# Another first phase for a fused attention and max-out kernel: order, weights' conversion, join of groups and first softmax

## The chip, the cores and the metric

The kernel runs on one core of a Trainium2 chip. The core has a matrix engine (PE, whose weight loads are shown apart as PEld), a vector engine (DVE), a scalar engine (ACT), a general engine (POOL) and a queue engine (SP) that here starts the transfers. Each engine works through a list of its own, in order, and waits where an instruction needs what another engine has not yet made. The metric is the device time of one execution in microseconds (us): 817.84, the median of three runs (817.79 to 818.44).

## What is computed

Four batches of 12544 tokens with 128 channels go through an attention with 32 learned queries, then through a feed-forward layer that takes the largest of three products. Cut to what matters:

```python
I = broadcast(inducing, (B, 32, 128))
def mab(q, kv):
    s = scale * (q @ kv.T); s = s - s.max(-1)
    a = exp(s); a /= a.sum(-1) + 1e-09
    return a @ kv
h = mab(I, x)                 # 32 states per batch, over all 12544 tokens
y = mab(x, h)                 # every token looks at the 32 states
f = max(y @ w1, y @ w2, y @ w3)   # 128 -> 768
out = f @ w_out                   # 768 -> 128
```

x is float32. The four weights are float64; the kernel reads their two 32-bit words (low, high) and makes float32 of them on the chip.

## The kernel before

A batch's 98 tiles of 128 tokens are seven groups: group 0 has 2 tiles, groups 1 to 6 have 16. Because `y @ w` is `a @ (h @ w)`, the kernel multiplies the 32 states with the weights once per batch (tile `us`, taken apart into a high and a low half so that a fast product keeps its digits) and then works on chunks of at most 512 tokens. For each chunk there are six steps ("slots"), one for each 128 of the 768 middle channels. In a slot PE makes `pu` (product with w1 - w2) and `pv` (with w3 - w2), ACT makes `ru = max(pu, 0)`, DVE makes `h = max(pv, ru)`, ACT casts h to `hi`, POOL (for a few slots DVE) makes `lo = h - hi`, and six slots later PE adds three products with w_out's two halves to the chunk's accumulator `acc`. `pu` and `pv` have two banks each, `ru` has three buffers. One call of `advance` (L813) issues pu of one slot, pv of the one before, and relu, cast and maximum in their turn.

All that comes before is the first phase: the four weights have to be converted, and the first batch's states computed, before the first slot can start. For each group k of the first batch the steps are: load x (SP), transposes in four pieces (T, PE, L282), copies of these from PSUM (c, ACT, L288), scores (S, L298), maximum over the tokens (M, DVE, L308), spread of the maximum over the four quarters (D on ACT, G on PE), least (L, DVE, L327; maxima are kept negated), exponential (E, ACT, L338), its transpose (R, DVE, L352), sum of x with these weights (U, PE, L366) and a copy of the sum (H, ACT, L379). Then the groups are joined: each sum is scaled by the factor of its own maximum (K, `add_group`, on POOL and DVE), two products bring them together (`pa`, `sum`, L610), and the state hT comes out of one DVE product (L635).

A weight is converted in six passes over 128 x 768 words (`convert`, L182; `measure`, L177, squares the high word on ACT to find numbers too small to keep): shift, sign, exponent, low word times exponent, sum (POOL for w1 and w3, DVE for w2 and w_out), and a product that clears the small ones. Then w1 - w2 and w3 - w2 (L219).

The order of all this is written by hand: `STEPS1` (L43) is a list of steps that are issued one after the other, each of which puts its instructions at the end of its engines' lists, `F` being products of an identity that nobody reads. `ORDER` (L55) goes on with the softmax of the first tokens, in two parts (a: group 0 and 4 tiles of group 1, b: the other 12 tiles of group 1), the first products with the weights, and the first seven calls of `advance` (s); S there is the scores of group 2. From then on `main` (L1044) goes from slot to slot by a plan. In slot 8 the plan has the first scores for the second batch (`turn_products`, L389).

LOADS (L41) is the order of the transfers: 0 to 6 are groups of x, 7 is w2, 8 w_out, 9 w1, 10 w3.

## Time and profile before

| | |
|---|---|
| median of three runs | 817.84 us |
| span of the profiled execution, first to last instruction | 816.4 us |
| PE busy | 806.8 us (99%) |
| ACT busy | 720.2 us (88%) |
| POOL busy | 658.8 us (81%) |
| DVE busy | 653.4 us (80%) |
| granted clock of PE | 1.000 |

Times in the rows are us from the first instruction of that execution. The median of the runs stands 1.4 us above its span. A share of busy time is a mean over very different stretches: the first 55 us are one piece of work that happens once, the other 760 us repeat the slot. A step of the first phase is found in the timeline by its line. PE's fp32 products show as two records for each, and the pieces of one tile are merged in a row with their count (x8 for eight transposes).

### The profile page before, as it was taken

Reading aid. Unit: us, or ns where it says so; the run is one execution under the profiler, and the core shown is the slowest. Engines: PE = TensorE matmul, PEld = TensorE weight load, DVE = VectorE, ACT = ScalarE, POOL = GpSimd, SP = SyncE. Lnnn points to the kernel's source line nnn. Section 1 sums busy time; section 2 is a strip of 40 time slices with the busy share of each in tenths; the row PEclk is TensorE's granted clock in tenths of the full one; section 3 lists DMA queues with packets and bytes.
Section 4 is the critical chain, followed back from the end, with each engine's and each line's share of the span. In section 5 each row is a group of like instructions: output and inputs, shape, how many; then the busy total and the mean of one; then the engine's idle time right before and its main releaser. Section 6 shows DMA issues by size and latency. Waiting matters only on the chain.

```text
span 816.4 us, 14999 instructions
## 1 busy us (share of the span) xinstructions
PE 806.8 (99%) x4565; PEld 628.9 (77%) x4565; DVE 653.4 (80%) x1198; ACT 720.2 (88%) x1446; POOL 658.8 (81%) x640
## 2 busy tenths in 40 slices
PE   8999999999999999999999999999999999999998
PEld 5667778777787787777777877877778778777886
DVE  5989778787797797887986978878789878878874
ACT  5779889898898898988988988989889999999996
POOL 0369898798798987987989888879878888878886
PEclk9999999999999999999999999999999999999999
DMA  9335643543553435435453354343231222222221
GB/s 345 140 149 160 192 150 107 182 125 105 155 175 123 129 107 176 124 112 177 128 166 112 114 167 124 110 126 124 60 108 56 83 65 79 69 81 75 62 78 52
DMA packets 45408, 101.47 MB, mean 124 GB/s; under 512 B 9360, under 2 KB 15376, under 8 KB 40208
## 3 DMA queue, kind: packets, MB, share of 16 engines
q1 hardware_dynamic: 45184, 100.39, 39.1%
q8 instruction: 36, 0.59, 0.3%
q14 instruction: 44, 0.36, 0.1%
q10 hardware_dynamic: 144, 0.13, 0.0%
HBM read 48.12 MB, written 25.69 MB: 90 GB/s over the span
## 4 chain that ended last, share of the span: by engine, by line
PE 94%; DVE 3%; ACT 1%; issue 1%; DMA 1%; POOL 0%; SPq 0%; DVEq 0%
PE acc L908 49%; PE pv L826 16%; PE pu L820 16%; PE aux L708 3%; PE acc L904 3%; PE acc L486 2%; PE aux L389 2%; DVE h L858 1%; DMA xg<-in_x_dram 1%; POOL rest L208 0%; PE pv L282 0%; PE pu L282 0%; PE aux L298 0%; PE aux L670 0%; ACT ru L835 0%
## 5 line engine op out<-in xcount | busy, mean ns | idle before, releaser
L850 POOL TENSOR_TENSOR lo<-h,hi 128x512 fp32r<-128x512 f32 (+1 forms) x498 | 624.8, 1284 | 109.3 <-ACT hi L842 58.4
L858 DVE TENSOR_TENSOR h<-pv,ru 128x512 f32<-128x512 f32 (+1 forms) x524 | 349.9, 672 | 131.2 <-PE pv L826 106.7
L835 ACT ACTIVATE ru<-pu 128x512 f32<-128x512 f32 (+1 forms) x600 | 365.3, 609 | 66.8 <-PE pu L820 61.8
L842 ACT CAST hi<-h 128x512 fp32r<-128x512 f32 (+1 forms) x524 | 326.5, 623 | 3.0 <-DVE h L858 2.2
L908 PE MATMUL acc<-hi,wo_hi 128*128 128x512 f32 (+1 forms) x601 | 235.1, 391 | 0.0
L826 PE MATMUL pv<-pT,us 128*128 128x512 f32 (+1 forms) x600 | 233.0, 389 | 1.0 <-DVE h L858 0.8
L820 PE MATMUL pu<-pT,us 128*128 128x512 f32 (+1 forms) x600 | 231.8, 386 | 0.1
L908 PE MATMUL acc<-hi,wo_lo 128*128 128x512 f32 (+1 forms) x601 | 231.5, 385 | 0.0
L908 PE MATMUL acc<-lo,wo_hi 128*128 128x512 f32 (+1 forms) x601 | 231.4, 385 | 0.0
L908 PEld LDWEIGHTS acc<-hi,wo_hi 128*128 128x128 f32 x601 | 112.8, 188 | 41.8 <-issue 20.5
L826 PEld LDWEIGHTS pv<-pT,us 128*128 128x128 f32 x600 | 112.6, 188 | 28.6 <-DVE h L858 5.5
L820 PEld LDWEIGHTS pu<-pT,us 128*128 128x128 f32 x600 | 112.6, 188 | 24.5 <-ACT ru L835 1.7
L908 PEld LDWEIGHTS acc<-lo,wo_hi 128*128 128x128 f32 x601 | 112.8, 188 | 23.0
L908 PEld LDWEIGHTS acc<-hi,wo_lo 128*128 128x128 f32 x601 | 112.9, 188 | 21.8
L858 DVE TENSOR_TENSOR aux<-pv,ru 128x512 f32<-128x512 f32 x66 | 45.9, 695 | 11.6 <-PE pv L826 4.5
L861 DVE TENSOR_TENSOR lo<-aux,hi 128x512 fp32r<-128x512 f32 x66 | 45.4, 688 | 0.8 <-PE acc L908 0.8
L842 ACT CAST hi<-aux 128x512 fp32r<-128x512 f32 x66 | 40.5, 614 | 0.3
L920 ACT COPY shelf<-acc 128x512 f32<-128x512 f32 (+1 forms) x65 | 39.0, 600 | 0.0
L904 PE MATMUL acc<-pT,us 128*128 128x512 f32 (+1 forms) x100 | 38.8, 388 | 0.0
L208 POOL TENSOR_TENSOR rest<-rest,t 128x768 f32<-128x768 f32 x2 | 3.7, 1826 | 28.7 <-DVE rest L204 23.6
L430 POOL COPY mq<-mq 32x1 f32<-32x1 f32 (+2 forms) x108 | 20.4, 189 | 5.2
L708 PE MATMUL aux<-xT,hT 128*32 128x512 f32 x184 | 24.5, 605 | 0.0
(169 smaller groups left out, 561.6 us busy)
## 6 DMA issues: line engine op xcount, KB each, us to landing
out_dram<-shelf SPq DMA_DIRECT2D x95, 256.0 KB, 2.0
xg<-in_x_dram SPq DMA_DIRECT2D x22, 1024.0 KB, 5.8
xT<-in_xt_dram SPq DMA_DIRECT2D x18, 1024.0 KB, 5.1
pT<-ph SPq DMA_DIRECT2D x184, 64.0 KB, 2.0
pT<-pl SPq DMA_DIRECT2D x184, 64.0 KB, 2.0
raw<-in_w_dram SPq DMA_DIRECT2D x3, 768.0 KB, 13.5
us<-uh SPq DMA_DIRECT2D x24, 52.0 KB, 2.4
us<-ul SPq DMA_DIRECT2D x24, 52.0 KB, 1.9
```

The lines of the kernel that those rows point to most:

```text
L430: nc.gpsimd.tensor_copy(out=far[to : to + step], in_=own[lo : lo + step])
L708: nc.tensor.matmul(out=sp[q * M : (q + 1) * M, :w], lhsT=st["hT"][:, :M], rhs=xT[:, q * w : (q + 1) * w], start=True, stop=True)
L820: nc.tensor.matmul(out=pu[:, :w], lhsT=state[c.b]["us"][:, 2 * j * P : (2 * j + 1) * P], rhs=c.pT[:, :w], start=True, stop=True)
L826: nc.tensor.matmul(out=pv[:, : d.w], lhsT=state[d.b]["us"][:, (2 * j + 1) * P : (2 * j + 2) * P], rhs=d.pT[:, : d.w], start=True, stop=True,)
L835: nc.scalar.activation(out=ru[:, :w], in_=pu[:, :w], func=AF.Relu)
L842: nc.scalar.copy(out=hi[:, : c.w], in_=h[:, : c.w])
L850: nc.gpsimd.tensor_sub(**args)
L858: nc.vector.tensor_max(out=h[:, : d.w], in0=pv[:, : d.w], in1=relus.pop(s)[:, : d.w])
L861: nc.vector.tensor_sub(**low)
L904: nc.tensor.matmul(out=c.acc[:, :w], lhsT=us[:, 2 * DF :], rhs=c.pT[:, :w], start=True, stop=False)
L908: nc.tensor.matmul(out=c.acc[:, cs], lhsT=lhs[:, j, :], rhs=rhs[j][:, cs], start=False, stop=(j == NJ - 1 and rhs is c.hl and cs.stop == w),)
L920: (nc.vector.tensor_copy if by_vector else nc.scalar.copy)(out=o[:, : c.w], in_=c.acc[:, : c.w])
```

## The change

The hand-written lists `STEPS1` and `ORDER` are replaced by one list, `HEAD`, which also runs slots 0 to 7; `main` starts at slot 8. What the list issues changes too:

- Weights: the high word's size is taken by Abs on ACT (`weight_size`, n), DVE makes a small number of the low word (`weight_rest`, r), raises the size to a least value (`weight_least`, m) and shifts its bits (`weight_shift`, i), POOL adds the two as whole numbers (`weight_whole`, v; all four weights), and DVE puts the sign on (`weight_sign`, d).
- Transfers: groups 1 and 2 come ahead of w2, and w_out is the last of the eleven (it was the fifth).
- Unread products: 17 at the start and none until the first products with the weights; then, in a bank of `pv`, ten of 256 columns in six pieces, before and between the first calls of `advance` (N).
- Copies: four of the copies of transposed x (C) and one copy of a group's sum (HV, group 1) go from ACT to DVE; all seven sums are kept in SBUF.
- Join: one product makes seven masks from the factors (`combine_masks`, DVE), and seven small products on PE (`combine_group`, y) add the groups; the adds on POOL and DVE go.
- First softmax: three parts (A: group 0, B: 4 tiles of group 1, C: the other 12), the first and second chunk's probabilities being turned by `probs_turn` and copied by DVE and ACT.
- The scores of group 2 go from `ORDER` into the plan, to slot 8.

Three places of the lists show what moves. First PE's list from its first instruction, where acc<-ident_r is an unread product, pu and pv the banks of the transposes, xg_86 group 1 and xg_87 group 2. Before:

```order
L274 MATMUL acc_76<-ident_r 128x384 x4
L282 MATMUL pu_72<-shelf 128x128 x2
L274 MATMUL acc_76<-ident_r 128x384
L298 MATMUL aux_70<-shelf 32x64 x4
L274 MATMUL acc_76<-ident_r 128x384 x2
L321 MATMUL acc_76<-md,shelf 128x4
L282 MATMUL pu_72<-shelf,xg_86 128x128 x4
L282 MATMUL pu_73<-shelf,xg_86 128x128 x4
L282 MATMUL pv_74<-shelf,xg_86 128x128 x4
L282 MATMUL pv_75<-shelf,xg_86 128x128 x4
L274 MATMUL acc_76<-ident_r 128x384 x2
L298 MATMUL aux_71<-xT_78,shelf 32x512 x4
```

After:

```order
L271 MATMUL acc_76<-ident_r 128x384 x17
L279 MATMUL pu_72<-shelf 128x128 x2
L279 MATMUL pv_74<-shelf,xg_86 128x128 x4
L279 MATMUL pv_75<-shelf,xg_86 128x128 x4
L279 MATMUL pu_73<-shelf,xg_86 128x128 x4
L295 MATMUL aux_70<-shelf 32x64 x4
L279 MATMUL pu_72<-shelf,xg_86 128x128 x4
L279 MATMUL pv_74<-shelf,xg_87 128x128 x4
L279 MATMUL pu_73<-shelf,xg_87 128x128 x4
L318 MATMUL acc_76<-md,shelf 128x4
L295 MATMUL aux_71<-xT_78,shelf 32x512 x4
```

The unread products are all ahead of the first transpose, and transposes of group 2 come ahead of the scores of group 1 (aux_71).

Second, PE's list at the first slots, where L820 and L831 are pu, L826 and L837 pv, L789 and L795 the turning of probabilities, and aux_70<-xT,hT the scores of group 2. Before:

```order
L789 MATMUL pu_72<-ident_r,pn 128x128 x2
L649 MATMUL acc_76<-shelf,hT 128x128
L789 MATMUL pu_73<-ident_r,pn 128x128 x4
L820 MATMUL pu_72<-pT,us 128x256
L708 MATMUL aux_70<-xT_79,hT 32x512 x4
L820 MATMUL pu_73<-pT,us 128x256
L826 MATMUL pv_74<-pT,us 128x256
L820 MATMUL pu_72<-pT,us 128x256
L826 MATMUL pv_75<-pT,us 128x256
```

After:

```order
L271 MATMUL pv_74<-ident_r 128x256 x2
L795 MATMUL pu_72<-ident_r,pn 128x128 x2
L657 MATMUL acc_76<-shelf,hT 128x128
L795 MATMUL pu_73<-ident_r,pn 128x128 x4
L831 MATMUL pu_72<-pT,us 128x256
L271 MATMUL pv_74<-ident_r 128x256 x2
L831 MATMUL pu_73<-pT,us 128x256
L837 MATMUL pv_74<-pT,us 128x256
L271 MATMUL pv_74<-ident_r 128x256 x2
L831 MATMUL pu_72<-pT,us 128x256
L837 MATMUL pv_75<-pT,us 128x256
L271 MATMUL pv_74<-ident_r 128x256
```

The scores of group 2 are gone from here, and unread products stand between a pv and the next pu, in the bank of that pv.

Third, ACT's list from the cast of the last softmax part (pn, 128x24x32 values) on, where ru is the relu and hi the cast of h. Before:

```order
L765 CAST pn<-aux_71 128x24x32
L800 CAST pT<-pu_73 128x4x4x32
L835 ACTIVATE ru<-pu_72 128x256
L654 CAST us<-acc_76 128x128
L662 COPY uf<-acc_76 64x128
L835 ACTIVATE ru<-pu_73 128x256
L835 ACTIVATE ru<-pu_72 128x256
L842 CAST hi<-h 128x256
L835 ACTIVATE ru<-pu_73 128x256
L842 CAST hi<-h 128x256
```

After:

```order
L853 CAST hi<-h 128x256
L846 ACTIVATE ru<-pu_73 128x256
L853 CAST hi<-h 128x256
L846 ACTIVATE ru<-pu_72 128x256
L853 CAST hi<-h 128x256
L846 ACTIVATE ru<-pu_73 128x256
L853 CAST hi<-h 128x256
L774 CAST pn<-acc_77 128x24x32
L846 ACTIVATE ru<-pu_72 128x512
L853 CAST hi<-h 128x256
```

The cast of pn stood ahead of the first relu; it now stands between the relus of 256 and of 512 columns.

The diff, cut to its core:

```diff
-LEAST = 2.0**-15 * 1.125
+LEAST = 2.0**-15
...
-    LOADS = (0, 7, 1, 2, 8, 3, 4, 9, 5, 10, 6)
+    LOADS = (0, 1, 2, 7, 3, 9, 4, 5, 10, 6, 8)
...
-    STEPS1 = (
-        "F4 T0.0 c0.0 F1 S0 M0 D0 F2 G0 W0 z0 W0 T1.0 W0 T1.1 c1.0 L0 W0 E0 T1.2 c1.1 R0 T1.3 W0 "
...
+    HEAD = """
+        F:17 T:0.0 T:1.2 T:1.3 T:1.1 C:0.0 S:0 T:1.0 c:1.2 T:2.2 c:1.1 T:2.1 M:0 D:0 G:0 L:0 C:2.1 c:1.3 c:1.0 S:1
...
+        turn:0 pcv:0 up:3 hi:3 turn:1 pca:1 s:0 lop:3 p:2.4 lov:2 N:2 s:1 N:2 s:2 p:2.5 N:1 s:3 N:1 s:4 p:2.6 N:2
+        s:5 p:2.7 next s:6 p:2.8 q:0 q:1 q:2 q:3 q:4 q:5 q:6 q:7
...
-    ORDER = "a a b a a b a b 0 w l a b a a b b 1 2 a b p c b P s X 3 Y S z s s s s s b s"
...
-        size = sizes[k] = hp.tile([P, DF], F32, name="size", tag="size", bufs=2)
-        nc.scalar.activation(out=size, in_=high.bitcast(F32), func=AF.Square)
...
+    def weight_size(k):
         v = raws[k].rearrange("p (k two) -> p two k", two=2)
+        words[k] = v[:, 0, :], v[:, 1, :]
+        sized[k] = hp.tile([P, DF], F32, name="size", tag="size", bufs=2)
+        nc.scalar.activation(out=sized[k], in_=words[k][1].bitcast(F32), func=AF.Abs)
+    def weight_rest(k):
+        rests[k] = hp.tile([P, DF], F32, name="rest", tag="rest", bufs=2)
+        low = raws[k].rearrange("p (k two) -> p two k", two=2)[:, 0, :]
+        nc.vector.tensor_scalar(out=rests[k], in0=low, scalar1=2.0**-51, scalar2=2.0, op0=ALU.mult, op1=ALU.add)
+    def weight_least(k):
+        nc.vector.tensor_scalar(out=sized[k], in0=sized[k], scalar1=LEAST, scalar2=None, op0=ALU.max)
+    def weight_shift(k):
+        bits = sized[k].bitcast(U32)
+        nc.vector.tensor_scalar(out=bits, in0=bits, scalar1=3, scalar2=None, op0=ALU.logical_shift_left)
+    def weight_whole(k):
+        whole = rests[k].bitcast(I32)
+        nc.gpsimd.tensor_tensor(out=whole, in0=whole, in1=sized[k].bitcast(I32), op=ALU.add)
+    def weight_sign(k):
+        floats[k] = wf[:, k, :] if k < 2 else hp.tile([P, DF], F32, name="dst", tag="dst", bufs=2)
+        nc.vector.scalar_tensor_tensor(
+            out=floats[k].bitcast(U32),
+            in0=words[k][1],
+            scalar=0x80000000,
+            in1=rests[k].bitcast(U32),
+            op0=ALU.bitwise_and,
+            op1=ALU.bitwise_or,
         )
...
-            out=t, in0=high, scalar1=3, scalar2=0x3FFFFFF8, op0=ALU.logical_shift_left, op1=ALU.bitwise_and
-            out=t, in0=high, scalar=0xC0000000, in1=t, op0=ALU.bitwise_and, op1=ALU.bitwise_or
-        nc.vector.tensor_scalar(out=pw, in0=t, scalar1=0xFF800000, scalar2=None, op0=ALU.bitwise_and)
-            out=rest, in0=low, scalar=2.0**-52, in1=pw.bitcast(F32), op0=ALU.mult, op1=ALU.mult
-        (nc.gpsimd if k > 1 else nc.vector).tensor_add(out=rest, in0=rest, in1=t.bitcast(F32))
-            out=dst, in0=sizes[k], scalar=LEAST * LEAST, in1=rest, op0=ALU.is_ge, op1=ALU.mult
...
-    def attend_keep(b, gi):
+    def attend_keep(b, gi, copy):
-        nc.scalar.copy(out=st["hg"][:parts, gi, :], in_=st["h"][:parts, :C])
+        copy(out=st["hg"][:parts, GROUPS.index(gi), :], in_=st["h"][:parts, :C])
...
+            "HV": lambda gi: attend_keep(0, gi, vec.tensor_copy),
+            "N": lambda n: unread_products(n, bank_v[0][:, 2 * P :]),
...
+    def combine_masks(st, engine):
+        st["mask"] = bp.tile([P, NG, M], F32, name="mask", tag="mask", bufs=1)
+        engine.tensor_mul(
+            out=st["mask"],
+            in0=sel[:, :M].unsqueeze(1).to_broadcast([P, NG, M]),
+            in1=st["w"].unsqueeze(2).to_broadcast([P, NG, M]),
+        )
...
+    def combine_group(st, at, bank):
+        st["sum"] = bank
+        parts = min(groups[GROUPS[at]]["nt"], NQ) * M
+        nc.tensor.matmul(
+            out=bank[:, :M],
+            lhsT=st["hg"][:parts, at, :],
+            rhs=st["mask"][:parts, at, :],
+            start=(at == 0),
+            stop=(at == NG - 1),
+        )
...
+    PARTS = (("A", groups[0]["nt"]), ("B", TC), ("C", GT - TC))
+
+    def scores_part(which):
 
         st = state[0]
+        gi = int(which > 0)
+        xT, per = st["xT"][gi], groups[gi]["nt"] * M
+        key, bank, a, z = (
+            ("A", bank_v[0], 0, per), ("B", bank_a[0], 0, TC * M), ("C", bank_o[1], TC * M, per)
+        )[which]
...
-        total = (bank_a[0] if gi == "A" else bank_a[1])[:, 512 - GT : 512 - GT + nt]
+        total = sp[:, w : w + nt] if gi in ("A", "B", "C") else bank_a[1][:, 512 - GT : 512 - GT + nt]
...
+    def probs_turn(c, bank):
         src = state[c.b][("p", c.key)]
+        c.pT = wk.tile([P, 512], F32R, name="pT", tag="pT", bufs=4)
+        for t in range(c.w // P):
+            nc.tensor.transpose(
+                out=bank.bitcast(F32R)[:, t * P : (t + 1) * P],
+                in_=src[:, c.base + t, :, :, :].rearrange("p d s m -> p (d s m)"),
+                identity=ident_r,
+            )
...
-            if i > 0:
-                at(s0 + BURST[0], scores_products, b, g + 1, bank_a[0])
+            at(s0 + BURST[0], scores_products, b, g + 1, bank_a[0])
...
-        phase1_first()
...
+        head()
+        main(8)
```

## Rows read from the trace of the kernel before

**Rows 1.** Page: us busy, share of the span and instructions of each engine.

```profile
PE 806.8 (99%) x4565; PEld 628.9 (77%) x4565; DVE 653.4 (80%) x1198; ACT 720.2 (88%) x1446; POOL 658.8 (81%) x640
```

**Rows 2.** Windows: stretch, us, busy PE PEld DVE ACT POOL, clock, DMA, GB/s.

```profile
10.00:25.00 15.00, 14.49 (x128) 9.28 (x127) 11.86 (x19) 11.34 (x25) 0.00 (x0) 1.00 1.02 408
14.90:41.06 26.16, 24.63 (x335) 17.15 (x333) 24.22 (x47) 20.20 (x48) 7.80 (x9) 1.00 0.52 200
41.06:55.27 14.21, 13.51 (x88) 8.32 (x88) 12.48 (x31) 11.30 (x29) 8.13 (x10) 1.00 0.54 211
55.27:75.00 19.73, 19.73 (x110) 14.74 (x111) 17.16 (x35) 17.83 (x37) 18.18 (x20) 1.00 0.26 86
```

**Rows 3.** Chain that ended last: start, us, what; 0 to 70 us.

```profile
24.14 0.97 DVE rest L204
...
25.18 1.84 POOL rest L208
...
51.67 0.28 ACT ru L835
51.95 0.29 ACT hi L842
```

**Rows 4.** Timeline, first feed-forward steps: start, us, engine, line, op, tiles, count.

```profile
47.40 0.80 ACT L765 CAST pn<-aux 128x768 fp32r<-128x768 f32 x1 [0.45 <-DVE aux L759]
...
48.05 1.06 PE L708 MATMUL aux<-xT,hT 128*32 128x512 f32 x8
...
48.57 0.40 ACT L835 ACTIVATE ru<-pu 128x256 f32<-128x256 f32 x1
...
54.53 0.68 DVE L802 CAST pT<-acc 128x512 fp32r<-128x512 f32 x1
...
55.27 0.16 PEld L389 LDWEIGHTS acc<-shelf 128*32 128x32 f32 x8 [0.72 <-DVE pT L802]
```

**Rows 5.** DVE groups, 0 to 48 us: busy us, mean ns, idle before.

```profile
L352 DVE STREAM_TRANSPOSE aT<-a 128x512 f32<-128x512 f32 x6 | 4.2, 707 | 0.5 <-ACT a L338 0.5
L308 DVE TENSOR_REDUCE mq<-aux 128x1 f32<-128x512 f32 x6 | 4.1, 684 | 2.6 <-PE aux L298 2.6
...
L195 DVE SCALAR_TENSOR_TENSOR t<-raw,t 128x768 uint32<-128x768 uint32 x4 | 3.8, 959 | 0.1
L200 DVE TENSOR_SCALAR pw<-t 128x768 uint32<-128x768 uint32 x4 | 2.2, 560 | 0.1
...
L219 DVE TENSOR_TENSOR shelf<-dst,xT 128x768 f32<-128x768 f32 x1 | 1.0, 960 | 0.0
L327 DVE TENSOR_REDUCE mneg<-acc 128x1 f32<-128x4 f32 x6 | 0.9, 156 | 0.2 <-PE acc L321 0.2
```

**Rows 6.** Groups of ACT and POOL, 0 to 48 us, in the same form.

```profile
L288 ACT COPY xT<-pu 128x512 f32<-128x512 f32 x12 | 6.9, 601 | 3.6 <-PE pu L282 3.6
...
L208 POOL TENSOR_TENSOR rest<-rest,t 128x768 f32<-128x768 f32 x2 | 3.7, 1826 | 28.7 <-DVE rest L204 23.6 <-DVE mneg L327 5.1
```

**Rows 7.** Timeline of DVE: the least of group 1, and the state hT.

```profile
14.90 0.16 DVE L327 TENSOR_REDUCE mneg<-acc 128x1 f32<-128x4 f32 x1 [0.25 <-PE acc L321]
...
40.77 0.29 DVE L635 TENSOR_TENSOR hT<-pu,rec 128x128 f32<-128x128 f32 x1
```

**Rows 8.** Timeline of PE: unread products, and runs of eight transposes.

```profile
1.88 1.65 PE L274 MATMUL acc<-ident_r 128*128 128x384 f32 x4 [1.88 <-DVE ident_r L154]
...
7.09 1.97 PE L282 MATMUL pu<-shelf,xg 128*128 128x128 f32 x8 [0.17 <-DMA xg<-in_x_dram]
...
12.95 1.09 PE L282 MATMUL pu<-shelf,xg 128*128 128x128 f32 x8
...
28.88 1.09 PE L282 MATMUL pu<-shelf,xT 128*128 128x128 f32 x8
```

**Rows 9.** DMA issues of 5 to 6 us and of 9.44 to 11 us.

```profile
xg<-in_x_dram SPq DMA_DIRECT2D x1, 1024.0 KB, 11.1
...
xT<-in_x_dram SPq DMA_DIRECT2D x1, 256.0 KB, 17.2
```

More of the change, by code (lines that the diff above doesn't have):

```diff
@@ L11 @@
 U32 = mybir.dt.uint32
-LEAST = 2.0**-15 * 1.125
+I32 = mybir.dt.int32
+LEAST = 2.0**-15
 AF = mybir.ActivationFunctionType
@@ L126, in place @@
         return shelf[:, shelf_at[0] - n : shelf_at[0]]
-    outs = [place(512) for _ in range(OB)]
+    join = place(OB * 512)
+    outs = [join[:, i * 512 : (i + 1) * 512] for i in range(OB)]
     short_t = [place(groups[0]["nt"] * P) for i in range(2)]
@@ L141 @@
     raws = {}
-    FULL = next(gi for gi in LOADS if 0 < gi < NG)
+    FULLS = [gi for gi in LOADS if 0 < gi < NG]
     def first_loads():
@@ L226, with weight_difference @@
+    def weight_difference(k, part, parts, engine):
+        js = range(part * NJ // parts, (part + 1) * NJ // parts)
+        cs = slice(js[0] * P, (js[-1] + 1) * P)
+        engine.tensor_sub(
+            out=wcat[:, : 2 * DF].rearrange("p (j s c) -> p s j c", s=2, c=P)[:, k - 2, js[0] : js[-1] + 1],
+            in0=floats[k][:, cs].rearrange("p (j c) -> p j c", c=P),
+            in1=wf[:, 0, cs].rearrange("p (j c) -> p j c", c=P),
+        )
     w2t = []
@@ new lines, in head @@
+            "pcv": lambda n: probs_copy(chunks[n], bank_u[n], vec.tensor_copy),
+            "s": lambda n: advance(),
+            "q": slot,
+        }
+        for step in HEAD.split():
+            name, *args = step.split(":")
+            args = [int(a) for a in ".".join(args).split(".")] if args else []
+            if name in "TcC" and len(name) == 1:
+                if name == "T":
+                    transpose_x(0, *args)
+                else:
+                    copy_x(0, *args, act.copy if name == "c" else vec.tensor_copy)
+            elif name in ("e", "ep"):
+                weight_difference(*args, vec if name == "e" else pool)
+            elif name == "p":
+                which, n = args
+                if which not in softmax:
+                    softmax[which] = scores_steps(0, *PARTS[which])
+                next(softmax[which])
+            elif name in ("parts", *steps):
+                steps[name](*args)
+            else:
+                raise ValueError(step)
@@ L1107, with main @@
+    def main(first):
+        for s in range(first, len(slots) + LAG + 1):
+            slot(s)
+    with tc.manual_schedule(engines=MANUAL):
+        head()
+        main(8)
 _GT = 16
```

335 lines of the change are left out of this document (119 added, 216 removed), and 7 rows, old and new, of the table STEPS1.

## The prediction

> **What bounds the kernel now.** The page first [rows 1]: PE is busy for 806.8 of 816.4 us, every other engine for under 90%. The windows come next [rows 2]: from 55.27 us on PE has no gap (19.73 of 19.73), so what lies behind 55.27 costs the same however early it starts. A change of the first phase is therefore worth exactly the time by which it moves the product that stands at 55.27 (L389, the first scores of the second batch, slot 8 of the feed-forward steps), as long as PE's list behind it stays the same, and it does. Third, the chain in order of time [rows 3] says what holds that product back. Up to the state hT it runs through the weights' conversion on DVE and POOL (rows at 24.14 and 25.18, and the same again for the next weight); the window 14.90 to 41.06 agrees, with DVE busy 24.22 of 26.16, more than ACT (20.20). From 51 us on the chain alternates between ACT's relu (0.28) and cast (0.29), and in the end stands DVE's copy of probabilities (54.53), which L389 waits for [rows 4]. So there are two stretches: 14.90 to hT's end at 41.06 (DVE), and 41.06 to 55.27 (14.21 us, mostly ACT).
>
> **First stretch: the conversion and the join.** Before, a weight costs DVE two passes of 0.56 (L191, L200) and three of 0.96 (L195, L204, L212), and a fourth of 0.96 (L208) for w2 and w_out; POOL adds for the other two [rows 5, 6]. After, it is three of 0.56 (rest, least, shift) and one of 0.96 (sign): 2.64 for each against 4.96 or 4.00, or 10.6 against 17.9 in all. Against that stand new DVE instructions: of 24 copies of transposed x of 128x512, 3 go from ACT to DVE (0.68 each, as the copy at 54.53 in [rows 4]), one copy of a group's sum (128x128), and one product of 128x224 for the masks, while the joins of L581, L583 and L604 go. Of the old 17.9, w2's whole 4.96 was done before 14.90; of the new passes only one is, since w2 now lands behind two groups of x.
>
> So I count what DVE has to do between the least of group 1 (14.90 before, [rows 7]) and hT, with the durations of [rows 5]: 11 single-input passes at 0.56 = 6.2; 4 sign passes at 0.96 = 3.8; one difference of 128x768 at 0.96 = 1.0; 6 transposes at 0.707 = 4.2; 5 maxima at 0.684 = 3.4; 2 copies at 0.68 = 1.4; 6 least at 0.156 and three of that size = 1.4; and six smaller ones (copy, mask, half a difference, two for the reciprocal, hT's own 0.29) about 2.2. Sum 23.6.
>
> Where does it start? Group 1 no longer stands behind w2 in the queue; PE is with the 17 unread products until about 7.3 (1.88 plus 17 of 384 columns at 1.2 GHz, 0.32 each; the row of four at 1.88 took 1.65 [rows 8]). If the clock is up after them, the 16 transposes of group 1 cost twice 1.09 (row at 12.95) in place of twice 1.97 (row at 7.09): 1.7 us less, of which the start, later by 0.2, and ACT's copies of 0.6 take about half. I put the least of group 1 at 14.1. The later groups don't hold it up: 768 KB less lie ahead of group 3 (issued at 5.08, landing 11.1 later, [rows 9]) and of group 6 (first quarter at 26.6), which is 1.9 us at the 408 GB/s of [rows 2]: 14.3 and 24.7.
>
> 14.1 + 23.6 = 37.7 would be hT's end without any wait. Before, DVE waited for 1.94 us of the 26.16. After, I find waits where the queue stands: the copy of group 1's sum (put on DVE, ahead of the least of group 2) waits for PE's scores of groups 2 and 3 and that sum, and so does all behind it, ACT's weights of group 2 included; the fourth weight's sign, just ahead of hT, waits for POOL's add. About 0.9 in all, so **hT ends at 38.6: 2.45 earlier**. From below it is 37.7 (no wait), from above 39.7 (waits as before). The unknown prices: an integer add on POOL, taken like the fp32 add (1.83), is covered by some 0.5 us of other DVE work for w1, w3 and w_out, so up to 2.3 it costs nothing; Abs in place of Square on ACT and max or shift on DVE keep the shapes of rows at hand and are taken at those; the mask lies between a 128x128 and a 128x384 pass (0.3 to 0.6; I take 0.37, and it is off by at most 0.2).
>
> **Second stretch, hT to L389.** Four terms against the 14.21 of before.
> (a) The cast of the big part's probabilities (0.80, with ACT idle for 0.45 ahead of it, row at 47.40 [rows 4]) no longer stands ahead of the first relu; a copy uf of 512 columns (0.6, as ACT's copies in [rows 6]) is new there. 0.45 + 0.80 - 0.6 = **0.6 gained**.
> (b) That cast now stands between the fourth and fifth cast of h, in the chain of relus and casts that sets this stretch, with nothing to cover it: **0.8 lost**.
> (c) The unread products write the bank of pv that DVE reads for h, so PE's queue stands until h is made, and the next pu is queued behind. The relu for that slot could start when h of two slots before is done (its buffer), now h, two products of 256 columns, pu and the way to ACT come after each other: about **0.65 lost**, once; the second such place is covered by ACT's queue.
> (d) The scores of group 2 (1.06, row at 48.05 [rows 4]) stood where PE waited for the second chunk's probabilities. Now they stand in slot 8, ahead of L389, where PE waited 0.72 for DVE (row at 55.27): 1.06 less the part of that wait which is left, about **0.4 lost**.
> The three softmax parts give nothing more: the first pu needs parts A and B, whose DVE passes interleave with C's.
> Sum: 14.21 - 0.6 + 0.8 + 0.65 + 0.4 = 15.46, so L389 comes at 38.6 + 15.46 = 54.05 and not 55.27: 1.2 us earlier. The profiled execution's span of 816.4 becomes 815.2; the median of the runs, 817.84, stands 1.4 above the span, and with the same 1.4 the forecast is **816.6**. Bounds of the terms: (b) and (c) between 0 (covered) and 0.8 and 1.3 (both places), (d) 0 to 1.06.
>
> **A rule against the change.** The row at 7.09 shows a run of transposes alone, on a PE that had been busy for most of the time since 1.88, at half the rate of the row at 12.95 (the granted clock reads 1.00 in every window, so the level is read from durations); between the two rows stand unread products and scores. The Trainium skill, "TensorE: Matmul & The Clock Gate", Part 4 (PE-mode transpose), says that transposes don't count as busy for the clock the way other products do; the trace agrees as far as that row goes. It is rival 2, whose price comes from the rows alone. Of POOL's add, the Trainium skill, "GPSIMD Engine Reference", Key points, says that POOL shares its SBUF interfaces with DVE and gets into its way in DVE's two-port modes; the add of 1.83 was measured beside such passes, and no row here shows it without.
>
> **Rivals.**
> 1. *Nothing is given back.* The relus and casts still set the pace, but (b), (c), (d) fall into waits that I don't see; hT at 38.6 or a little before. 817.84 - 2.45 = 815.4, with hT at 37.7 814.5; I say 814.9. For it: ACT is at 11.30 of 14.21 in that stretch, so 2.9 us are free. Against: the chain at 51.67 and 51.95 has no gap.
> 2. *The clock falls (slower).* Before, seven pieces of unread products stand among the transposes of the first groups; after, all 17 are ahead of the first transpose and from 7.3 to about 16 PE has almost only transposes, and waits for group 3. If the clock falls there, the 16 transposes of group 3 cost 1.8 more (twice 1.97 for 1.09), the scores of groups 2 and 3 and the sum of group 1 about 0.4 each: 3.0, on the way to DVE's maxima. It decides if the drop lasts beyond 14.3, when group 3 lands; earlier it is hidden by that transfer. 816.6 + 3.0 = 819.6. Against: the transposes at 28.88, with no unread product for many us ahead of them, keep 1.09 for 8, but they have scores and sums around them.
> 3. *The integer add on POOL is slow (slower).* At twice the fp32 price (3.7), w1's sign waits 1.4 longer and w_out's, ahead of hT, 1.4 again: 819.4. From 2.3 it starts to count.
> 4. *It doesn't do what it says:* hT is held by ACT's and PE's turn from maximum to weights, not by DVE; the waits grow by the 1.2 that are left. 817.8.
>
> **Chances.** Forecast 0.45 (own range 815.3 to 817.9), rival 1 0.25, rival 2 0.12, rival 3 0.08, rival 4 0.10. No change means within 0.2%, 1.6 us here: 816.2 to 819.5. Of the forecast's 0.45 some 0.17 lie below 816.2. Faster 0.17 + 0.25 = 0.42; same 0.28 + 0.10 = 0.38; slower 0.20. The range takes in rival 1 with its lower end and reaches to rival 2: 814.4 to 819.6.
>
> **What will show it.** The window from the least of group 1 to hT: hT's end near 38.6, DVE busy there for about 23.6. POOL's integer add at 1.8. The transposes of groups 1 and 3 at 1.1 for 8 (2.0: rival 2). ACT's cast of 128x768 between casts of h, and PE idle in front of the third unread pair with DVE's h as the releaser. L389 near 54. The forecast is wrong if hT stays above 40, or if L389 comes less than 14.5 us after it.

## The result, and the profile after

The changed kernel takes 822.62 us (median of five runs, 819.79 to 824.14) where the kernel before takes 818.2 (817.79 to 818.56): a ratio of 1.0053, 95% interval 1.0043 to 1.0064. It is slower by half a per cent. The forecast was 816.6, and its range ended at 819.6.

The five runs differ by more than those of before, and they differ with PE's mean granted clock, which was 0.998 once and otherwise 0.999 or 1.000 in the runs of the kernel before that were timed beside the experiments:

```
us       819.79  822.51  822.62  823.27  824.14
clock     1.000   0.995   0.996   0.995   0.993
```

The profiled execution is the one of 823.27 (span 821.5). First its windows, in the form of [rows 2]: from the least of group 1 to hT's end, a part of that, a part with a low clock, from hT to the first scores of the second batch (L380, in the kernel before L389), and what follows.

```profile
15.63:41.35 25.72, 24.07 (x328) 18.11 (x328) 23.24 (x45) 18.24 (x45) 7.32 (x4) 0.93 0.51 190
16.00:34.00 18.00, 17.94 (x248) 13.02 (x247) 17.27 (x32) 15.17 (x38) 5.50 (x3) 1.00 0.66 253
37.97:44.80 6.83, 6.45 (x64) 4.14 (x57) 4.50 (x17) 1.44 (x4) 0.00 (x0) 0.50 0.54 170
41.35:59.10 17.75, 16.08 (x99) 10.00 (x103) 12.96 (x37) 12.76 (x33) 9.74 (x11) 0.90 0.47 169
...
59.10:79.00 19.90, 19.90 (x115) 14.87 (x108) 16.69 (x35) 17.74 (x36) 18.04 (x20) 1.00 0.28 87
```

The stretch up to hT ends at 41.35, not at 38.6, and the next one takes 17.75, where the forecast had 15.46 and the kernel before 14.21 [rows 2]. Behind L380 PE has no gap, as before. So L380 comes at 59.10, 3.83 later than in [rows 4], and that is most of the 5.1 by which the span grew. Note that PE was busy for 17.94 of the 18.00 us from 16 to 34.

Then DVE's timeline around hT, and POOL's add (start, us, engine, line, operation, tiles). The product of weights and group sums, `lw`, has seven columns and takes 1.77; it ends when POOL's integer add ends (34.98 + 1.82 = 36.80).

```profile
34.75 0.38 DVE L608 TENSOR_TENSOR mask<-shelf,w 128x224 f32<-128x224 f32 x1
...
35.05 1.77 DVE L627 TENSOR_TENSOR lw<-w,lst 128x7 f32<-128x7 f32 x1
...
41.06 0.29 DVE L643 TENSOR_TENSOR hT<-pu,rec 128x128 f32<-128x128 f32 x1 [1.68 <-PE pu L617]
```

```profile
34.98 1.82 POOL L201 TENSOR_TENSOR rest<-rest,size 128x768 int32<-128x768 int32 x1 [4.22 <-DVE size L197]
```

Two more of DVE's passes are long: `rest` at 18.04 and the sign at 22.88 take 1.15 and 1.46, where the same passes take 0.55 and 0.94 elsewhere. Both start while POOL adds (16.94 to 18.77 and 21.70 to 23.53) and end behind it.

```profile
18.04 1.15 DVE L190 TENSOR_SCALAR rest<-raw 128x768 f32<-128x768 uint32 x1
...
22.88 1.46 DVE L205 SCALAR_TENSOR_TENSOR xT<-raw,rest 128x768 uint32<-128x768 uint32 x1
```

PE's timeline shows the rest: a wait for group 3's transfer at 15.83, a wait for the reduction behind `lw` at 37.07, the sums of one group in 1.08 at full clock and in 1.82 at 37.78, and later the two pieces of unread products (a pair and a single one) that wait for DVE's h.

```profile
15.83 0.66 PE L279 MATMUL pu<-shelf,xg 128*128 128x128 f32 x4 [0.24 <-DMA xg<-in_x_dram]
...
34.47 1.08 PE L359 MATMUL acc<-xg,aT 128*32 128x128 f32 x32 [0.35 <-ACT a L331]
...
37.07 0.41 PE L633 MATMUL acc<-shelf,l 128*128 128x32 f32 x2 [0.40 <-DVE l L629]
37.78 1.82 PE L359 MATMUL acc<-xT,aT 128*32 128x128 f32 x32 [0.30 <-DVE aT L345]
...
51.31 0.51 PE L271 MATMUL pv<-ident_r 128*128 128x256 f32 x2 [0.59 <-DVE h L869]
...
53.05 0.39 PE L271 MATMUL pv<-ident_r 128*128 128x256 f32 x1 [0.64 <-DVE h L869]
```

The granted clock in short windows: PE is busy for 0.65, 1.00 and 0.67 us of the three microseconds from 34, and from 38 on it gets half its clock (1.2 GHz in place of 2.4), until 44.8.

```profile
34.00:35.00 1.00, 0.65 (x22) 1.00 0.00 0
35.00:36.00 1.00, 1.00 (x25) 1.00 0.06 16
36.00:37.00 1.00, 0.67 (x6) 1.00 0.00 0
...
37.50:38.00 0.50, 0.22 (x8) 0.96 0.00 0
38.00:38.50 0.50, 0.50 (x17) 0.50 0.00 0
```

### The profile page after: what moved, and what is told of

Same layout as the page of the kernel before. It is cut to its first block, busy times and chain, and to the rows that moved or that the text cites. A ratio compares the mean times of both kernels' runs of the same rounds, so it can differ in the third digit from the quotient of the medians.

```text
span 821.5 us, 15091 instructions
## 1 busy us (share of the span) xinstructions
PE 809.9 (99%) x4584; PEld 632.4 (77%) x4584; DVE 648.3 (79%) x1200; ACT 717.6 (87%) x1445; POOL 658.9 (80%) x635
## 4 chain that ended last, share of the span: by engine, by line
PE 94%; DVE 3%; DMA 1%; ACT 1%; issue 0%; POOL 0%; SPq 0%; DVEq 0%; ACTq 0%
PE acc L919 49%; PE pv L837 16%; PE pu L831 16%; PE aux L716 3%; PE acc L915 3%; PE acc L477 2%; PE aux L380 2%; DMA xg<-in_x_dram 1%; DVE h L869 1%; PE aux L295 0%; PE acc L359 0%; PE pv L279 0%; DVE aT L345 0%; POOL lo L861 0%; PE aux L678 0%
## 5 line engine op out<-in xcount | busy, mean ns | idle before, releaser
L837 PE MATMUL pv<-pT,us 128*128 128x512 f32 (+1 forms) x600 | 233.5, 389 | 1.1 <-DVE h L869 0.9
L831 PE MATMUL pu<-pT,us 128*128 128x512 f32 (+1 forms) x600 | 231.9, 387 | 0.1
L919 PEld LDWEIGHTS acc<-hi,wo_hi 128*128 128x128 f32 x601 | 112.8, 188 | 41.4 <-issue 20.5
L837 PEld LDWEIGHTS pv<-pT,us 128*128 128x128 f32 x600 | 112.6, 188 | 30.2 <-DVE h L869 7.2
L831 PEld LDWEIGHTS pu<-pT,us 128*128 128x128 f32 x600 | 112.7, 188 | 23.7 <-ACT pT L524 0.3
L915 PE MATMUL acc<-pT,us 128*128 128x512 f32 (+1 forms) x100 | 38.8, 388 | 0.0
L201 POOL TENSOR_TENSOR rest<-rest,size 128x768 int32<-128x768 int32 x4 | 7.3, 1829 | 28.2 <-DVE size L197 28.2
L716 PE MATMUL aux<-xT,hT 128*32 128x512 f32 x184 | 24.5, 605 | 0.0
```

The source lines that it names most:

```text
L716: nc.tensor.matmul(out=sp[q * M : (q + 1) * M, :w], lhsT=st["hT"][:, :M], rhs=xT[:, q * w : (q + 1) * w], start=True, stop=True)
L831: nc.tensor.matmul(out=pu[:, :w], lhsT=state[c.b]["us"][:, 2 * j * P : (2 * j + 1) * P], rhs=c.pT[:, :w], start=True, stop=True)
L837: nc.tensor.matmul(out=pv[:, : d.w], lhsT=state[d.b]["us"][:, (2 * j + 1) * P : (2 * j + 2) * P], rhs=d.pT[:, : d.w], start=True, stop=True,)
L915: nc.tensor.matmul(out=c.acc[:, :w], lhsT=us[:, 2 * DF :], rhs=c.pT[:, :w], start=True, stop=False)
L919: nc.tensor.matmul(out=c.acc[:, cs], lhsT=lhs[:, j, :], rhs=rhs[j][:, cs], start=False, stop=(j == NJ - 1 and rhs is c.hl and cs.stop == w),)
```

## The experiments

The changed kernel's list HEAD can be edited step by step (v is POOL's integer add, i the shift ahead of it, d the sign; 1 stands for w_out). Every kernel below is the changed kernel with the edits shown, timed beside the kernel before. hT is the end of that pass and L380 the start of the first scores of the second batch, both in the profiled execution, with its mean clock; the ratio is that of the times to the kernel before. There is one profiled execution of each kernel, and hT and L380 vary from execution to execution (f4's is the slowest of its twelve, 824.21), so the median says what an edit is worth and the profile why.

```
                        ratio    interval         median   hT     L380   clock
changed kernel          1.0053   1.0043-1.0064    822.62  41.35  59.10   0.995
e1_sum_first            1.0021   1.0012-1.0030    819.71  40.13  57.91   0.997
e2_filler               1.0030   1.0021-1.0040    820.45  39.73  55.89   1.000
e3_no_unread_ffn        1.0024   1.0015-1.0033    820.44  40.76  57.59   0.993
e4_scores_first         1.0063   1.0050-1.0075    823.39  41.32  59.40   0.995
f1_add_early_filler     1.0027   1.0017-1.0036    820.04  41.47  58.00   0.998
f2_and_no_unread_ffn    1.0009   1.0000-1.0018    818.85  41.70  56.76   0.996
f3_and_scores_first     1.0027   1.0019-1.0036    820.21  41.24  56.33   0.998
f4_group2_in_head       1.0003   0.9988-1.0017    817.63  44.92  61.25   0.991
g4_sum_on_pool          1.0015   1.0006-1.0024    818.85  39.88  56.09   0.997
g2_unread_other_bank    1.0045   1.0031-1.0058    820.67  39.77  54.17   0.999
g1_four_edits           1.0002   0.9993-1.0011    818.13  39.32  54.14   0.999
g3_no_unread_ffn        0.9997   0.9989-1.0006    817.65  41.24  55.68   0.998
h3_w2_early             1.0069   1.0049-1.0090    825.24  44.75  62.67   0.996
h2_all_w2_early         1.0022   1.0013-1.0032    819.61  41.81  56.27   0.998
h1_all_scores_first     1.0033   1.0021-1.0045    820.60  42.83  57.28   0.997
```

### Does DVE's lw wait for POOL?

```diff
-i:1 v:1 mask lw w2T
+mask lw i:1 v:1 w2T
```

> Only one pass is moved: the shift of w_out's sizes (0.55 on DVE), and with it the start of POOL's integer add, goes behind the product of weights and group sums (lw, L627). Theory A (DVE's lw, both operands in SBUF, stood still while POOL added): lw takes 0.2 and not 1.77; PE's wait for the sum of the groups (0.40 at 37.07) goes, hT ends at 39.4 (41.35 with the change); if the clock then holds, L380 comes near 55.7 and the time is about 819. Rival (lw is slow by itself, or waits for ACT's weights): lw stays at 1.77 and hT at 41.3, time 822.6. Rival (the clock falls for want of unread products whatever DVE does): lw is short, hT ends near 40, but the granted clock reads 0.50 for some 7 us around 40, time about 821.

`lw` takes 0.16, and the difference that now meets the add takes 1.83 in place of 0.52. POOL ends at 38.22 and the difference at 38.64, nearly its usual length later:

```profile
35.44 0.16 DVE L627 TENSOR_TENSOR lw<-w,lst 128x7 f32<-128x7 f32 x1
...
36.81 1.83 DVE L217 TENSOR_TENSOR shelf<-dst,xT 128x384 f32<-128x384 f32 x1
```

```profile
36.41 1.81 POOL L201 TENSOR_TENSOR rest<-rest,size 128x768 int32<-128x768 int32 x1 [5.54 <-DVE size L197]
```

So the wait belongs to the add, not to `lw`: a pass of DVE with two operands in SBUF that comes while POOL adds stands still until the add is done. (`rest` at 18.04 shows that one of a single operand can stand still too.) Transposes and passes that read PSUM go on beside an add, as in the changed kernel beside the one from 28.92 to 30.75, the second of these lines being a maximum over PSUM:

```profile
29.51 0.71 DVE L345 STREAM_TRANSPOSE aT<-a 128x512 f32<-128x512 f32 x1
30.14 0.65 DVE L305 TENSOR_REDUCE mq<-aux 128x1 f32<-128x512 f32 x1
```

The time of e1 is 2.9 us lower than the changed kernel's; hT is only 1.2 earlier, and behind it, from 40 on, the clock fell in this execution as well (0.55 in the window from 40 to 42).

The other half of the same question takes `lw` off DVE and moves the difference behind the reciprocal, and changes nothing else:

```diff
-i:1 v:1 mask lw w2T ... tot e:3.0.2 rec
+i:1 mask lw v:1 w2T ... tot rec e:3.0.2
-        nc.vector.tensor_mul(out=lw, in0=st["w"], in1=st["lst"])
+        nc.gpsimd.tensor_mul(out=lw, in0=st["w"], in1=st["lst"])
```

> The changed kernel, with the product of weights and group sums (lw, 7 columns) made by POOL ahead of its integer add, and the difference e:3.0.2 behind the reciprocal, so that no pass with two SBUF operands that hT needs meets the add. Nothing else. Theory A: lw about 0.2 on POOL, DVE's transposes of the last group at 35.3 and not 36.94, the difference waits for the add's end (1.0 to 1.5 instead of 0.52) but ends before PE has the last group's sum; hT ends at 38.5 to 38.9, as the prediction had it (38.6). Whether the clock then holds is open: if it does, L380 at 54.9 and time about 817.9; if it falls, 820. Rival (PE's and ACT's turn holds hT anyway): hT not before 40.

hT ends at 39.88, but this execution had its least of group 1 only at 16.51, since the clock fell near 12 us (0.50 in the window from 12 to 14; more of this below). From there the stretch took 23.37. In `g2_unread_other_bank`, which has the changed kernel's code up to hT and kept its clock, it took 24.35 (15.42 to 39.77). Counted from PE's sums of the last group but one (34.26 in g2, 35.32 in g4), hT ends 5.51 and 4.56 later, so the wait of `lw` is worth 0.95 of hT. From g2's start of 15.42 the 23.37 would end at 38.8, an estimate, and that is where theory A had it. The rival was half right: with the wait gone, DVE stands waiting for PE (0.93 ahead of the reciprocal).

Bringing the add forward instead, with four unread products of 384 columns in the idle places:

```diff
-d:3 M:6 D:6 L:5 E:5 U:4 H:4 G:6 r:1 m:1 L:6 E:6 R:5 least wts i:1 v:1 mask lw
+d:3 r:1 L:5 m:1 i:1 v:1 M:6 D:6 E:5 U:4 H:4 G:6 L:6 E:6 R:5 least wts mask lw
-y:1 tot e:3.0.2        ...  y:6 hT
+y:1 X:1 tot X:2 e:3.0.2  ...  y:6 X:1 hT
```

> w_out's rest, least, shift and the POOL add go ahead of the last group's maximum, so that POOL adds beside DVE's maximum and transposes (which read PSUM or have one operand), not beside the mask, lw or a difference; four unread products of 384 stand between the joins. Theory A: lw 0.2, no pass of DVE between 33 and 40 is longer than its usual time, hT ends at 38.3 to 38.9, clock 1.00, L380 16.2 later (54.5 to 55.1); with the 1.3 that all kernels with the change are later behind L380, the time is about 818.7. Rival (the wait only moves on to another pass, as it did with the sum first: mask or difference grows to 1 or more): hT after 39.4, time 819.8 or more.

A miss. No pass of DVE between 33 and 40 is long any more (`lw` 0.16), yet hT ends at 41.47 with the clock at 1.00: the last group's maximum now stands behind 1.7 us of conversion, and PE waits 1.32 for what follows from it.

```profile
34.81 0.39 PE L318 MATMUL acc<-md,shelf 128*128 128x4 f32 x2 [1.32 <-ACT md L311]
```

### What is the clock worth, and what keeps it up?

Seven unread products between the joins ahead of hT, in a bank (aux0) that nobody reads there:

```diff
-y:1 tot e:3.0.2          ...  y:3 y:5 y:6 hT
+y:1 X:2 tot X:2 e:3.0.2  ...  y:3 y:5 X:2 y:6 X:1 hT
+            "X": lambda n: unread_products(n, bank_a[0][:, P:]),
```

> Seven unread products of 384 columns go into PE's list between the joins ahead of hT, in a bank that nobody reads there; lw is left as it is. Clock theory (PE's idle pieces between 34 and 38, 1.4 in all, make the clock fall from 37.97 to 45.3): the granted clock stays 1.00, hT ends at about 39.9 and L380 comes 2.7 to 3.3 earlier than 59.10; time about 819.8, as the one run of the changed kernel whose mean clock read 1.0. Rival (the clock falls for another reason, or PE is still idle for long): clock 0.50 for 7 us again, time 822 to 823. Under both, lw stays at 1.77.

In nine runs the mean clock was never below 0.998 (0.993 to 1.000 in the five of the changed kernel), the median is 2.2 lower, and `lw` still takes 1.78. L380 comes 3.2 earlier, at the upper end of what was expected. So the clock's part is shown twice: by this kernel, and by the spread of runs of one kernel. `g2_unread_other_bank` had 817.83 at a mean clock of 0.999 and 822.19, twice, at 0.993. Its profiled execution had much the same pauses (PE busy 0.74, 1.00 and 0.60 of the microseconds from 34) and kept the clock, so pauses of this size let it fall in most executions, not in all. The wait of `lw` has a share in it: the kernels that have it and no filler (the changed kernel, e3, e4, g2) kept a mean clock of 0.998 or more in 5 of 26 runs, the two without it and without filler (e1, g4) in 18 of 22, and e2, with the wait and the filler, in 9 of 9. What decides in the single case isn't settled.

### What do the unread products between the first steps cost?

```diff
-hi:2 N:2 turn:0 ... lov:2 N:2 s:1 N:2 s:2 p:2.5 N:1 s:3 N:1 s:4 p:2.6 N:2 s:5
+hi:2 turn:0 ... lov:2 s:1 s:2 p:2.5 s:3 s:4 p:2.6 s:5
```

> The ten unread products of 256 columns between the first feed-forward steps are left out (their results are read by nobody). Theory (they make PE wait for DVE's h, rows at 51.31 and 53.05, 0.59 and 0.64, at both places): both waits go and the stretch from hT to L380 is 1.2 to 1.8 shorter than 17.75; time about 821.2. Rival (ACT's chain of relus and casts sets this stretch anyway): under 0.4 shorter, 822.4. Rival (they hold the clock up there): granted clock below 1.00 between 48 and 60, time above 823.

PE's two waits for h are gone and the stretch takes 16.83, with a clock that fell for longer (0.50 in the whole of 38 to 46). With the products kept but written elsewhere:

```diff
-            "N": lambda n: unread_products(n, bank_v[0][:, 2 * P :]),
+            "N": lambda n: unread_products(n, bank_a[1][:, : 2 * P]),
```

> The changed kernel, with its ten unread products between the feed-forward steps written to a bank that DVE's h does not read (aux1), at the same places. Theory (what costs is the wait for h that the bank brings, not PE's time): PE's two waits (0.59 and 0.64) go, as without the products; stretch from hT to L380 0.9 to 1.2 shorter than 17.75, the same gain as without them. Rival (their time on PE, some 0.2 to 0.4 at a place, costs as much): under 0.4 shorter. Clock at 38 as in the changed kernel: it falls; time about 821.5.

Both waits go as well, and in the profiled execution, at full clock, the stretch takes 14.40. `e2_filler` has the products in pv, also at full clock, and takes 16.16. The bank costs 1.76 (`g4_sum_on_pool`, with the products in pv and full clock there, takes 16.21). The products themselves cost little: of the two kernels below that differ in them alone, g1 with products in the other bank takes 14.82 and g3 without them 14.44, both at full clock. g2's row:

```profile
39.77:54.17 14.40, 14.13 (x99) 9.39 (x103) 12.95 (x38) 12.64 (x34) 9.76 (x11) 1.00 0.58 216
```

The median is 820.67, since in four of its five runs the clock fell. On top of `f1_add_early_filler`, leaving the products out:

> As f1_add_early_filler, and the ten unread products between the first feed-forward steps left out. Theory: their two places cost 1.2 in the stretch from hT to L380 (16.2 to 15.0), whatever the clock did before; L380 at 53.5, time about 817.5. Rival (in the run without them alone the gain was 0.9 only because the clock was low there; ACT's chain sets the stretch at full clock): under 0.5 earlier than f1, 818.4.

The median falls by 1.2, as the theory had it, to 818.85; the L380 expected (53.5) was missed, because hT was late as in f1 and the clock fell twice in this execution.

### Where group 2's scores stand

f2's edits, and:

```diff
-turn:1 pca:1 s:0 lop:3
+turn:1 pca:1 s:0 SP lop:3
+            "SP": lambda: scores_products(0, 2, bank_a[0]),
+            if i > 0:
                 at(s0 + BURST[0], scores_products, b, g + 1, bank_a[0])
```

> As f2_and_no_unread_ffn, and the scores of group 2 (1.06 on PE) go back from slot 8, ahead of L380, to the place behind the first step's products, where the kernel before had them. Theory: the first products wait for ACT there anyway, and the 0.4 to 1.06 in front of L380 is saved: L380 about 0.5 earlier than in f2, time about 817.0. Rival (the second step's products come 1 later and ACT's chain behind them): L380 the same as in f2 or up to 0.5 later, 817.5 to 818.

The median is 817.63, 1.2 under f2. But f2's five runs with a clock of 0.999 or more have 817.35 to 818.55 (median 817.79) and f4's ten 816.94 to 818.28 (817.59), so most of the 1.2 is the clock. The forecast's 0.4 for this term is not measured apart: these runs give 0.2 between their medians, while in single executions at full clock g1, with these scores at their old place, takes 14.82 from hT to L380 and g2, with them in slot 8, 14.40 (the two differ in edits ahead of hT as well).

### Is the first stretch held by group 1's start, by DVE, or by PE?

```diff
-c:1.2 T:2.2 c:1.1 T:2.1 M:0 D:0 G:0 L:0 C:2.1 c:1.3 c:1.0 S:1
+c:1.2 c:1.1 M:0 D:0 G:0 L:0 c:1.3 c:1.0 S:1 T:2.2 T:2.1 C:2.1
```

> The scores of group 1 go ahead of the two sets of transposes of group 2, whose transfer PE waits for (1.16 at 11.56). Theory: the least of group 1 comes at about 14.4 and not 15.63, and since DVE has no gap from 22.5 to 39.4, 0.5 to 1.2 of it reaches hT, if the moved start doesn't lay other DVE passes beside POOL's adds; time about 822. Rival (group 2 is later in exchange, and DVE waits there): hT unchanged within 0.3, time 822.6.

A miss: the least of group 1 came at 16.12. DVE's copy of group 2 (C:2.1) and the first transposes still stood ahead of group 1's maximum, and the copy now waited for its products. With these behind the maximum too, on top of f2:

```diff
+... S:1 T:2.2 T:2.1 E:0 M:1 D:1 C:2.1 R:0 n:0 T:2.3 c:2.3 G:1 L:1 T:2.0 U:0 r:0
```

> As f2_and_no_unread_ffn, and group 1's scores, maximum and squared term go ahead of everything of group 2 on PE and on DVE (the maximum ahead of DVE's copy of group 2 and of the first transposes, which held it up when only PE's order was changed). Theory: the least of group 1 at 14.2 and not 15.4; DVE is busy without gap from 22 to 34, so 0.4 to 1.0 reaches hT; time about 816.9. Rival (group 2 and 3 are later in exchange): hT within 0.2 of f2's, 817.5.

The least of group 1 comes at 13.69, earlier than expected, and nothing of it reaches hT (41.24). PE waits for group 3's transfer instead, for 1.71, up to the same 16 us as in the changed kernel:

```profile
13.89 0.41 PE L359 MATMUL acc<-shelf,aT 128*32 128x128 f32 x4
16.01 0.66 PE L279 MATMUL pu<-shelf,xg 128*128 128x128 f32 x4 [1.71 <-DMA xg<-in_x_dram]
```

The next three take work off DVE: w2 is loaded ahead of group 1, as before, and converted while the groups land. First in the changed kernel alone (its steps for w2 further back go; twelve unread products stand ahead of the first transposes and eight behind them):

```diff
-    LOADS = (0, 1, 2, 7, 3, 9, 4, 5, 10, 6, 8)
+    LOADS = (0, 7, 1, 2, 3, 9, 4, 5, 10, 6, 8)
-F:17 T:0.0 T:1.2 T:1.3 T:1.1 C:0.0 S:0 T:1.0 ... L:0 C:2.1
+F:12 n:0 r:0 m:0 i:0 v:0 T:0.0 C:0.0 S:0 F:8 T:1.2 T:1.3 T:1.1 T:1.0 ... L:0 d:0 C:2.1
```

> The changed kernel with w2 loaded ahead of group 1, as before, and converted while the groups land (size, rest, least, shift, add, sign: 3.2 of DVE's work before 14 us); twelve unread products ahead of the first transposes and eight between them and group 1's. Nothing else. Theory (DVE's work sets the first stretch): 2.6 of passes and the waits beside w2's add (0.6 at 18.04, 0.5 at 22.88) leave it; group 1 lands 1.9 later, but groups 2 and 3 do not; hT ends 2 to 3 earlier than at the same clock now: 37 to 38 at full clock, 38.5 if it falls. Time 820 (clock falling) or 818 (holding). Rival (landing of the groups and the turn of ACT and PE set it): hT at 39.5 or later at full clock, 41 if it falls; time 822.

Slower by 2.6: hT at 44.75. PE stood idle for 2.68 ahead of 8.94, since DVE's copy of group 0 was queued behind w2's passes, which waited for the transfer, and the whole first phase moved back. So hT was missed by its start: the least of group 1 came at 19.43. The stretch behind it took 25.32, where the changed kernel took 25.72, both with a fallen clock. The same with the edits of g3 (below):

> As g3_no_unread_ffn (sum on POOL, difference later, fillers ahead of hT, no unread products between the first steps, group 2's scores behind the first step), with w2's load and conversion early as in h3. Theory: hT at 37 to 38 where g3 had 39.3 to 41.2 depending on the start; L380 at 52; time about 815.7, faster than the kernel before by 0.25%. Rival: hT 39 or later, time 817.6 as g3.

Here the end can be read, beside g3, which differs in w2's place and in where the first unread products stand. DVE is busy for 14.87 of 18 us and PE for 17.87 (g3: 17.31 and 17.81), and the stretch from the least of group 1 to hT takes 23.92 (g3: 24.13), both at full clock. Taking 2.4 us off DVE made the stretch 0.2 shorter. First h2, then g3:

```profile
17.89:41.81 23.92, 23.37 (x333) 17.26 (x331) 19.01 (x41) 18.27 (x45) 5.85 (x4) 1.00 0.44 155
18.00:36.00 18.00, 17.87 (x248) 12.81 (x245) 14.87 (x30) 15.37 (x38) 3.66 (x2) 1.00 0.53 198
```

```profile
17.11:41.24 24.13, 23.51 (x333) 17.30 (x331) 21.65 (x44) 18.20 (x45) 7.67 (x5) 1.00 0.48 176
17.50:35.50 18.00, 17.81 (x245) 12.73 (x244) 17.31 (x32) 15.08 (x38) 5.49 (x3) 1.00 0.58 221
```

> As h2, and group 1's scores and maximum ahead of group 2's transposes and copy. With group 1 landing 1.9 later than in f3, group 2 is there when it is wanted, so both orders cost the same within 0.3: 815.5 to 816. If the first maxima set DVE's pace, 0.5 to 1 faster than h2.

Neither: 1.0 slower than h2. Both h1 and h2 also show the clock fall at the start, after PE's wait of 2.9 near 6 to 8.5 (0.61 and 0.55 in the window from 8 to 10).

### All mended together

g1 has g4's edits, five fillers of e2's kind, g2's bank and f4's scores; g3 is g1 without the ten products.

> Four edits together: the sum on POOL and the difference later (as g4), five unread products of 384 in PE's idle places ahead of hT, the ten of 256 in another bank (as g2), the scores of group 2 back behind the first step. Theory: hT 38.5 to 39, stretch 14.4 to 15 (the prediction's 15.46 without c and d), L380 at 53.2 to 53.8, clock at 1.00: time about 816.4, faster than the kernel before. Rival (the clock falls in the second stretch, as in f1 and f2 at 52): 818 or more.

> As g1_four_edits, without the ten unread products. If PE's pauses between 48 and 52 make the clock fall at 52 (as in f2, where they were left out): mean clock 0.997 or less in most runs, and slower than g1 by 0.5 to 1.5. If the products bring nothing there: the same as g1 or up to 0.4 faster.

In g1's execution hT ends at 39.32 and L380 comes at 54.14, 1.13 earlier than in the kernel before, and that run took 817.74; but the median is 818.13. g3 has 817.65, and its interval (0.9989 to 1.0006) holds 1, as g1's and f4's do. The expected 816.4 was missed. The start varies from execution to execution (least of group 1 at 15.06 in g1's, 2.1 later in g3's): PE now waits for group 2's transfer early on (1.99 at 11.60 in g3), and in g3's execution, as in g4's, the clock fell just behind that wait, so that the scores of group 1 took 1.94 in place of 1.06. After waits of the same size it held in g2 (2.04) and f1 (1.90). A window of g3:

```profile
13.00:14.00 1.00, 1.00 (x8) 0.00 (x0) 1.00 (x3) 0.98 (x3) 0.00 (x0) 0.50 0.94 393
```

Nor does all of a gain at L380 reach the end: from L380 to the span's end it is 761.13 in the kernel before and 761.13 to 762.41 in the executions with the change (761.76 in g1's). Mean clocks are 0.998 to 1.000 with and without the ten products. No version was found that is measurably faster than the kernel before.

## Why the prediction was wrong

The first scores of the second batch were forecast at 54.05 and came at 59.10, 5.05 later. The traces at full clock split it (rounded to 0.01 each):

- **hT, +1.17.** Forecast 38.6; 39.77 in g2's execution, with the same code up to there and the clock at 1.00. Of this, 0.95 is the wait of `lw` (g4).
- **A later start, +0.21.** The least of group 1 at 15.63, in g2's execution at 15.42.
- **The clock, +1.37 and +1.59.** The stretch up to hT took 25.72 in place of g2's 24.35, and the second one 17.75 in place of the 16.16 of e2.
- **Term (c), +1.11.** Forecast 0.65, measured 1.76.
- **Terms (a), (b) and (d), -0.41.** 14.40 with the bank moved, where 14.21 - 0.6 + 0.8 + 0.4 = 14.81 was forecast.

Behind L380, PE's last product ends 758.24 later, 757.62 in the kernel before, and the span's end after it comes 0.65 later; with 1.77 in place of 1.4 between span and time that makes the 823.27. These last 1.6 were not looked into. The prediction had it that what lies behind costs the same however early it starts; it held only to 1.3 us.

By size, what failed is the clock: the sum put it at nothing, and it took 2.96 of the 5.05. Next come term (c), too small by 1.11, and POOL's add, put at nothing where the wait beside it cost 0.95.

**The step that failed first in the argument is the reading of what bounds the first stretch.** The prediction compared DVE's 24.22 busy of 26.16 with ACT's 20.20 and called the stretch DVE's. The same row [rows 2] has PE at 24.63, which is more. Of that, 2.9 were unread products that the change moved to the front, so PE too had less to do; but what is left stands in one list behind group 3's transfer. In the changed kernel PE has 0.06 free between 16 and 34, and h2 shows that with DVE at 14.87 of 18 only 0.2 is gained. So rival 4, which named ACT's and PE's turn, was right about PE. DVE's own work was even less than counted: 23.24 busy in the stretch, of which 0.6, 0.5 and 1.6 are the long passes, so about 20.5 in place of 23.6. The passes are those that were counted, and their durations without the long parts sum to 23.0; but neighbouring passes overlap in the record (one of 0.55 starts at 32.51, the next at 32.97), and a sum of durations takes that time twice. Counting PE's list from group 3's landing on would have given the right bound: 22.70 busy from 15.42 on in g2 (38.1), and its waits make the 39.77. In the number this step cost little, and that is luck: without the wait of `lw` the estimate for hT is 38.8, next to the forecast's 38.6, since the start was put 1.3 too early (15.42 in g2) and the stretch 1.1 too long (24.5; 23.37 in g4).

**The start** was put at 14.1, with group 3 landing at 14.3 and holding nothing up. It is 15.63, since the scores of group 1 stand behind group 2's transposes in PE's list and PE waits 1.16 for that transfer at 11.56; and PE waits for group 3 until 15.83. Moving group 1 forward (f3) only made that last wait longer.

**POOL's add** takes the 1.82 that was forecast, and "up to 2.3 it costs nothing" was wrong all the same. The prediction priced the add's length and asked only when its result is wanted, not who runs beside it. That the add of 1.83 "was measured beside such passes" misreads the trace: beside the two adds of before (25.18 and 32.13) DVE had transposes, passes from PSUM and one of 128x6 with a single operand. The trace of before had the evidence elsewhere, in passes longer than their kind. A difference of 128x384 took 0.77 there (0.55 at 40.98) beside a POOL add that ran from 38.32 to 38.78, and in the steady part a subtraction of two SBUF tiles, 0.67 to 0.69 in 24 cases, took 1.82 and 1.88 in two while POOL did the same. With one of its operands in PSUM it never took more than 0.69 in 76 cases, in the midst of POOL's too (0.69 at 639.80, POOL 639.63 to 640.92). Where DVE started just ahead of POOL (238.44 and 238.48), it was POOL's that took longer, 1.80 in place of 1.30. `lw` itself took 0.15, beside a POOL instruction with one tensor operand (36.51 to 37.11):

```profile
36.77 0.15 DVE L614 TENSOR_TENSOR lw<-w,lst 128x6 f32<-128x6 f32 x1
...
38.42 0.77 DVE L219 TENSOR_TENSOR shelf<-dst,xT 128x384 f32<-128x384 f32 x1
...
608.76 1.82 DVE L861 TENSOR_TENSOR lo<-h,hi 128x512 fp32r<-128x512 f32 x1 [0.19 <-ACT hi L842]
```

The prediction named the Trainium skill, "GPSIMD Engine Reference", Key points, for the port that POOL shares with DVE, and gave only half of its sentence: the page names DVE instructions in a two-port mode "or with two SBUF inputs". The rows agree with that half beside POOL's adds of two tensors, since `lw` and the differences have two SBUF inputs; the 0.15 of before shows no wait beside a POOL instruction with one. `rest` at 18.04 is a one-input pass of 0.55 that took 1.15; whether it runs in a two-port mode, no row shows.

**The clock** was rival 2, with a chance of 0.12, and in the changed kernel's execution it fell in another place than named. Between 7 and 16 us, with 17 unread products ahead and transposes behind, it held there: eight transposes at 16.33 took 1.04. In g3's and g4's executions, with the same list up to there, it did fall near the named place, from about 12 to 15 or 16 us. In the changed kernel it fell at 38, after the pauses that the wait of `lw` and the turn of the last group put into PE's list, where the kernel before had two pairs of unread products. These were counted as moved and not as missed: that is the step that put the largest term at nothing, and e2, which puts such products back, keeps the clock.

**Term (c)**: the mechanism was as described, with DVE's h as the releaser. Only its size was off: the second place was taken as covered by ACT's queue, and both count (0.59 and 0.64), with another 0.24 ahead of pv at 55.35. The cast of 128x768 stands between casts of h, as forecast.
